# A diffusion block on one core: gate multiplication moved from VectorE to GpSimd, later weight loads, moved quads, raised filler thresholds

## The chip, the cores and the metric

One core of a Trainium2 chip runs the kernel. The metric is device time in microseconds, the median of the runs. The engines are called PE (TensorE, matmul; its weight loads are listed as PEld), ACT (ScalarE), DVE (VectorE), POOL (GpSimd) and SP (SyncE, which here only issues transfers).

## The reference

An attention block and a gated MLP, each with a layer norm, a modulation and a gate computed from a condition vector `c`. 2048 tokens, 640 features, 32 heads of 20, 1536 hidden features, all bfloat16:

```python
mod = (_silu(c) @ w_mod).reshape(c.shape[0], 6, 1, -1)
sa, ca, ga, sb, cb, gb = (mod[:, 0].copy(), ..., mod[:, 5].copy())
h = _layernorm(x, axis=-1) * (1 + ca) + sa
x = x + ga * _A_ref(h, A_wqkv, A_wo)
h = _layernorm(x, axis=-1) * (1 + cb) + sb
x = x + gb * _B_ref(h, B_w_gate, B_w_up, B_w_down)
```

`_A_ref` is softmax attention over all tokens followed by `@ wo`; `_B_ref` is `((h @ w_gate) * (h @ w_up)) @ w_down`.

## The kernel before

The program is written by a planner. Python code builds tasks (an engine, a duration, dependencies, a priority, and sometimes a gate), a greedy simulation puts them into an order for each engine, and `emit_program` writes that order out with semaphores. On the chip every engine runs its list in order. So a constant of the planner, even a duration, can change the order of everything that follows.

**Tiling.** Queries are cut into seven chunks (`CHUNKS`): 512 tokens, then six of 256. In a chunk there are eight items of four heads each. For an item, PE computes scores in units of 512 columns, with four heads in the four row groups of the array (line 1522), and the exponential of a unit is taken in one of two ways.

- ACT takes two units at a time from PSUM and writes `PP` (line 1559). Two pairs of PSUM banks alternate, so that PE can fill one while ACT reads the other.
- A *quad* is four units that go to DVE and POOL instead. DVE writes each unit as a biased int16 into `DB` (line 1583), then builds two terms from the bits in `DSS` (lines 1615 and 1623, `M` and `EX`), and a product of the first term with `DB` is made either by DVE (line 1620) or in four pieces of 512 columns by POOL (line 1635). `QUADS` says how many quads each item of each chunk has.

PE multiplies `PP` and `DSS` with the values (line 2189). At the end of an item DVE transposes and inverts the sums (1715, 1721), POOL (or, for some, DVE) multiplies (1723), DVE transposes back into `OcT` (1732), and SP copies the rows into `Ocp` (1744).

**The suffix of a chunk** (`suffix(ci)`) is out-projection, layer norm and MLP, and it runs as filling work under the next chunk's scores. Its gates let each round of matmuls start only from some number of exponentials on, spread over a share `GATE_F[ci]` of the next chunk; its priorities are 1000 x (ci + 1) upwards, those of the out-projection 1500 lower. `g`, `progress` and `gstart` count exponentials: chunk `ci` starts at `gstart[ci]`, `NG` is their number.

**Weights of the MLP.** Gate and up weights come in twelve column blocks (`fc`) through three buffers `stg` (line 1929, issued by SP). For the last chunk ten of the twelve have buffers of their own, `stx`. The first `nsq` = 5 of these lie in the region of dead queries, the other five in the region of the earlier MLP tiles, so that their loads wait for the MLP of chunk 4. The gate of their loads is `gstart[NC - 1] + 1 + STX_G * fc`, with `STX_G` 3.

**Down weights.** They are loaded once into `wd` (1502), after the last projection has left the region, and multiplied there by the gate `gb` in twelve instructions (1505), one for each row block of 640 columns. All down-projections depend on these.

**Locks.** DVE instructions that use the SBUF port shared with POOL are marked `lk = 1`. The planner does not start them while a POOL task runs that is marked, and the other way round. A POOL task with `lk = 2` also looks ahead: it is not started if a marked DVE task would be ready more than `LKTOL` before its end, and it gets a dependency on the last marked DVE task.

**Fillers.** The planner keeps a sum of PE's activity over the last 3413 ns. Below `FILL_HARD`, and from 20000 ns of the plan on, it puts in matmuls whose result is not used (`zero_fill`, line 2520, adds zeros to an open sum; line 2548 writes a free bank). `HAM_MIN` is the activity below which the planner takes PE to run at half speed. Ahead of fillers, `HOLD` keeps PE free if scores are about to be ready. A value below `FILL_MIN` makes the planner prefer projection and MLP rounds over value matmuls. `STAGE` sets such constants anew for each of the 57 items; what an entry does not name falls back to the global value.

Of the kernel before, what the change touches and what calls it, by code (L numbers as in the profile page):

```python
# [7 lines left out]
ALU = mybir.AluOpType  # L8
# [23 lines left out]
STEAL_END = 66197.894  # L32
STEAL_GAP = 200
HAM_W = 3413.3
HAM_MIN = 3000.0
LKTOL = 300.0


# [92 lines left out]
class Sched:  # L131
# [221 lines left out]
def emit_program(nc, sched, nsem_dma=56):  # L353
# [121 lines left out]


CHUNKS = ((0, 512), (512, 256), (768, 256), (1024, 256), (1280, 256), (1536, 256), (1792, 256))
QUADS = ((0, 4, 3, 3, 3, 4, 4, 4), (1, 2, 1, 2, 1, 2, 1, 2), (2, 2, 1, 2, 2, 2, 1, 2), (2, 2, 2, 2, 2, 2, 2, 2), (2, 2, 1, 2, 2, 2, 1, 2), (2, 2, 1, 2, 2, 2, 1, 2), (2, 1, 2, 2, 2, 1, 2, 0))
SPLITJ = 1
QHALF = ((0, 0), (0, 0))  # L480
TB_GATE = 2
# [2 lines left out]
PV_KEEP = 2  # L484
# [20 lines left out]
GU_ONE = 1  # L505
XCONT = 0
T3_POOL = 1
STX_G, W_ISSUE = 3, 500.0
ZFILL = 1
LATE0, LATE1 = 24.0, 0.2  # L510
HEAD_OUT = 2
NPS = 4
# [22 lines left out]
PREEMPT = 0.0  # L535
PRE_M = 0.3
PV0N = 1
GATE_F = (1.3, 0.5, 0.5, 0.5, 0.5, 0.5, 1.0)
FILL_MIN = 4190.746
FILL_HARD = 3500.0  # L540
FILL_T0, FILL_TH, FILL_MINH = 2300.0, 17000.0, 7500.0
FILL_MODE = 'P'
DUP_MIN = 0.0
# [17 lines left out]
NTERM = 2  # L561

STAGE = {
    0: {"HOLD": 95, "PVMAX": 14, "LKTOL": 300.0, "X_LATE": -179.96, "FILL_MIN": 4462.4, "STEAL_GAP": 200, "PVCAP": 12, "PVTOL": 249, "XBACK": 0, "D_LATE": 16, "TPRIO": 0.75, "EAGER": 9, "PV_KEEP": 2, "XDPRIO": 1.343, "PVMIN": 2, "D_RES": 74, "X_HALF": 0.0},
    1: {"EAGER": 12},
    2: {"DL": 0.376, "XBACK": 4, "EAGER": 3, "X_HALF": 8.9, "HOLD": 90.5, "PVCAP": 11},
    3: {"PVTOL": 91.9, "X_HALF": -35.7, "HOLD": 100.3},
    4: {"PVMIN": 4, "FILL_MIN": 4884.9, "D_RES": 14},
    5: {"PVMIN": 1, "PVMAX": 10},
    6: {"STEAL_GAP": 189.7, "XBACK": 1, "PV_KEEP": 3},  # L570
    7: {"DL": 0.501, "EAGER": 12, "PVTOL": 68.2},
    8: {"PVCAP": 11, "EAGER": 11},
    11: {"DL": 0.443, "X_LATE": 182.1},
    12: {"DL": 0.459, "FILL_MIN": 3951.9, "PVMIN": 5},
    13: {"DL": 0.417, "HOLD": 87.3, "XBACK": 1},
    14: {"D_RES": 37, "FILL_MIN": 4680.6, "LKTOL": 213.0, "EAGER": 11, "D_LATE": 16},
    17: {"HOLD": 80.9, "PVMAX": 8},
    18: {"HOLD": 176.8, "D_LATE": 16},
    19: {"DL": 0.471, "X_HALF": 175.2, "PV_KEEP": 2, "HOLD": 92.4},
    20: {"DL": 0.391, "X_LATE": 12.3},  # L580
    21: {"HOLD": 78.5},
    22: {"EAGER": 9},
    24: {"DL": 0.464, "X_HALF": -92.0, "LKTOL": 267.1},
    25: {"DL": 0.549, "XBACK": 1},
    26: {"DL": 0.411, "FILL_MIN": 3312.8, "PV_KEEP": 2},
    27: {"DL": 0.473},
    28: {"PV_KEEP": 4, "LKTOL": 434.2},
    29: {"X_LATE": -60.4, "PV_KEEP": 3},
    30: {"PVCAP": 8},
    31: {"PV_KEEP": 3, "HOLD": 134.3},  # L590
    32: {"XBACK": 1, "PVMAX": 9, "PVCAP": 17, "PVMIN": 3},
    33: {"DL": 0.442, "X_LATE": -93.2},
    34: {"PV_KEEP": 1, "LKTOL": 261.2},
    35: {"HOLD": 49.4},
    36: {"DL": 0.524},
    37: {"XBACK": 1},
    38: {"PVMIN": 3, "LKTOL": 408.0, "X_LATE": 5.0},
    39: {"X_LATE": -98.7, "PVMAX": 8, "PVTOL": 316.5},
    41: {"X_HALF": 32.3},
    43: {"D_LATE": 13, "X_LATE": 7.1, "X_HALF": 111.5},  # L600
    50: {"FILL_MIN": 4782.5},
    51: {"X_LATE": -53.2, "PVCAP": 11},
    52: {"HOLD": 122.0, "PV_KEEP": 3},
    53: {"X_HALF": -11.3},
    55: {"FILL_MIN": 3839.7, "XBACK": 0, "X_HALF": -89.7, "HOLD": 83.7, "EAGER": 3},
    56: {"LKTOL": 370.4, "PVMIN": 5},
}
XHALF = 1
STG_G0, STG_G, XC_G = 12, -10, -20
X_LATE = -24.052  # L610
X_HALF = 0.0
# [10 lines left out]
def build_kernel(nc, A_x, A_wqkv, A_wo, B_x, B_w_gate, B_w_up, B_w_down, c, w_mod, out):  # L622
    S, D, H, DH = A_x.shape[1], A_x.shape[2], 32, 20
# [6 lines left out]
    NC = len(CHUNKS)  # L630
# [6 lines left out]
    sc = Sched()  # L637
# [64 lines left out]
    gab = alloc("gab", [128, 2, D], BF16)  # L702
# [51 lines left out]
    wd_sb = Sub(late_off, late_size).alloc("wd", [128, FT, D], BF16)  # L754
# [35 lines left out]
    if NALT:  # L790
# [6 lines left out]
        nsq, nsx = nsx, len(stx)  # L797
# [606 lines left out]
    def need(x):  # L1404
        return 13 + 10 * x
# [41 lines left out]
    ev_gb = gab_round(5, 1, need(WM_NEED + .55))  # L1447
# [54 lines left out]
    d_wd = dma("sp", 128 * FT * D * 2, lambda e: e.dma_start(wd_sb[:], wdv[:, :, :]), proj_last, prio=20)  # L1502
    t_wd = []
    for f_ in range(FT):
        t_wd.append(dvl(395, lambda e, f_=f_: e.tensor_tensor(wd_sb[:, f_, :], wd_sb[:, f_, :], gab[:, 1, :],
                                                                ALU.mult), [d_wd] + ev_gb, prio=2.45))
# [83 lines left out]
    for qi, (it, us) in enumerate(dquads):  # L1590
# [36 lines left out]
        if X_POOL and qi % X_POOL == X_POOL - 1 and qi < len(dquads) - X_LAST and all(  # L1627
                dquads[z][0] == it for z in range(qi, min(len(dquads), qi + X_TAIL + 1))):
            st_["xby"] = None
            for x in range(X_PIECES):  # L1630
# [5 lines left out]
                t = Task("pool", w * POOL_NS + 180.0, fxp, [tm, te], prio=2.0 + .1 * qi + .01 * x, name=f"XP.{qi}")  # L1636
# [15 lines left out]
            t = term(fx, [tm, te], TT_2X, "X", src=0, last=True)  # L1652
# [118 lines left out]
    def suffix(ci):  # L1771
# [36 lines left out]
        for tl in range(ntl):  # L1808
# [30 lines left out]
            t = t0 + tl  # L1839
# [80 lines left out]
        for fc in range(FT):  # L1920
            use_x = tail and fc < nsx
            wbuf, dm = [], []
            for w_, wv in enumerate((wgv, wuv)):
                cell = {}
                if use_x:
                    cell["t"] = stx[fc][:, w_, :, :]

                def f(e, wv=wv, fc=fc, cell=cell):
                    return e.dma_start(cell["t"], wv[:, :, fc * 128:(fc + 1) * 128])
                t = dma("sp", int(STG_B * 128 * KD * 128 * 2), f,  # L1930
                        (sfx_done["qdead"] if fc < nsq else first) if use_x else
                        kp_use if ci == 0 else [], prio=16 + ci + .01 * fc, dur=W_ISSUE,
                        gate=int(gstart[NC] - 40) if tail and not use_x else int(gstart[NC - 1]) + 1 + STX_G * fc if tail else max(0, gb + (STG_G0 if ci == 0 else STG_G)))
                if not use_x:
                    t.acq = [(sStg[w_], "s", 1)]

                    def on0(task, cell=cell, w_=w_):
                        cell["i"] = task.slots["s"]
                        cell["t"] = stg[cell["i"]][:, w_, :, :]
                    t.on_start = on0  # L1940
                wbuf.append(cell)
                dm.append(t)
# [102 lines left out]
        for tl in range(ntl):  # L2045
# [5 lines left out]
            for (c_, w) in cuts:  # L2051
# [10 lines left out]
                if tail and TAILX:  # L2062
# [6 lines left out]
                            prio=1))  # L2069
# [8 lines left out]
    for it in range(len(items)):  # L2078
        ci, j = items[it]
# [313 lines left out]
    def pick_pe(t):  # L2393
# [64 lines left out]
        sr = s_ready()  # L2458
        if HOLD and sr is not None and t < sr <= t + HOLD and ring() >= RINGLOW:
            return half_x(t)  # L2460
        if sc.recent(t) < FILL_HARD and t > 20000 and do_fill(t):
            return True
        if sc.recent(t) < FILL_MIN and ring() >= RINGLOW and pick_x(t, True):
            return True
# [161 lines left out]
```

## Time and profile before

| what | us |
|---|---|
| three runs | 805.65, 806.5, 809.9 |
| median | 806.5 |
| the profiled execution | 804.39 |
| its span, as the profile counts it | 802.6 |
| PE busy | 787.8 (98%), 16467 matmuls |
| ACT busy | 764.6 (95%) |
| DVE busy | 691.0 (86%) |
| POOL busy | 390.1 (49%) |

PE's share is modelled from pipelined matmuls and overstates it. The granted PE clock is 1.00 in each stretch of 20 us, 0.99 in the last. In the chain of waits, followed back from the last instruction, PE has 63% of the span, ACT 24%, DVE 8%: neither engine alone sets the time. The DMA engines are busy 95% of the first 20 us, then mostly 10 to 40%.

Idle time is told in the list of groups after the second bar, with the engine and line that ended most of it. The busy time by stage gives, for a stretch of the span, busy microseconds of each engine with the number of instructions in brackets. Times in the timeline and the chain are from the start of the span.

### The profile page before, as it was taken

How to read it: one execution, taken by the hardware profiler on the slowest of the kernel's cores; microseconds unless marked ns; L12 is line 12 of the kernel's file. 1: busy time of each engine (PE TensorE's matmuls, PEld its weight loads, DVE VectorE, ACT ScalarE, POOL GpSimd, SP SyncE). 2: the span in 40 equal slices, each digit the busy share in tenths (PEclk: the TensorE clock that was granted, in tenths of full speed). 3: DMA queues.
4: the chain of work that ended last, by engine and by line, in shares of the span. 5: the costliest groups of instructions: out<-in, count | busy, mean ns of one | idle time of the engine just before them, and what ended most of it. 6: DMA issues, size and time to landing. Idle time of an engine off the chain costs nothing.

```text
span 802.6 us, 37539 instructions
## 1 busy us (share of the span) xinstructions
PE 787.8 (98%) x16467; PEld 376.9 (47%) x16467; DVE 691.0 (86%) x1407; ACT 764.6 (95%) x848; POOL 390.1 (49%) x404
## 2 busy tenths in 40 slices
PE   8999999999999999999999999999999999999998
PEld 4433433332244334444555455554555555455567
DVE  7878887888979789997899999999999899898654
ACT  6899999999999999999999999999999999999951
POOL 3343546476455742457566455663543435465300
PEclk9999999999999999999999999999999999999999
DMA  9843212112232362110042304230431044527300
GB/s 299 245 118 93 52 52 72 53 30 80 84 96 65 85 186 54 29 42 23 23 106 54 72 16 114 54 74 15 115 88 39 24 112 103 109 71 148 87 22 18
DMA packets 154313, 64.65 MB, mean 81 GB/s; under 512 B 116951, under 2 KB 154151, under 8 KB 154151
## 3 DMA queue, kind: packets, MB, share of 16 engines
q1 hardware_dynamic: 153223, 61.10, 30.0%
q8 instruction: 131, 2.15, 1.1%
q10 hardware_dynamic: 928, 1.15, 0.4%
q14 instruction: 31, 0.25, 0.1%
HBM read 50.63 MB, written 8.99 MB: 74 GB/s over the span
## 4 chain that ended last, share of the span: by engine, by line
PE 63%; ACT 24%; DVE 8%; issue 3%; SPq 1%; DMA 0%; POOL 0%; DVEq 0%; ACTq 0%; POOLq 0%
ACT PP L1559 24%; PE ps_all L1522 21%; PE ps_all L972 17%; PE ps_all L2189 14%; PE ps_all L1232 4%; DVE DB L1583 3%; PE ps_all L968 3%; DVE DSS L1623 1%; PE ps_all L2548 1%; DVE DSS L1615 1%; SPq L1744 1%; DVE DSS L1620 1%; PE ps_all L2520 1%; PE ps_all L1129 1%; PE ps_all L1887 1%
## 5 line engine op out<-in xcount | busy, mean ns | idle before, releaser
L1559 ACT ACTIVATE PP<-ps_all 128x1024 bf16<-128x1024 f32 x810 | 747.5, 1097 | 5.2 <-PE ps_all L1522 2.9
L1635 POOL TENSOR_TENSOR DSS<-DB,DSS 128x512 bf16<-128x512 bf16 x288 | 327.3, 1157 | 301.0 <-DVE DSS L1623 239.2
L1583 DVE TENSOR_SCALAR DB<-ps_all 128x512 int16<-128x512 f32 x428 | 285.5, 681 | 49.1 <-PE ps_all L1522 47.2
L1522 PE MATMUL ps_all<-QT,KT 32*128 32x256 bf16 (+2 forms) x3648 | 317.5, 286 | 6.6 <-ACT PP L1559 2.1
L1522 PEld LDWEIGHTS ps_all<-QT,KT 32*128 32x128 bf16 x3648 | 93.4, 92 | 208.0 <-ACT PP L1559 143.8
L2189 PE MATMUL ps_all<-PP,Vf 128*32 128x256 bf16 (+2 forms) x2892 | 161.9, 290 | 0.3 <-DVE Vf L1321 0.2
L972 PE MATMUL ps_all<-h2T,stg 128*32 128x256 bf16 (+2 forms) x2692 | 125.0, 282 | 0.8 <-DVE DB L1583 0.4
L2189 PEld LDWEIGHTS ps_all<-PP,Vf 128*32 128x32 bf16 (+1 forms) x2892 | 55.0, 94 | 75.0 <-issue 66.3
L2189 PE MATMUL ps_all<-DSS,Vf 128*32 128x256 bf16 (+1 forms) x1512 | 87.9, 290 | 0.5 <-DVE DSS L1620 0.3
L972 PEld LDWEIGHTS ps_all<-h2T,stg 128*32 128x32 bf16 x2692 | 61.2, 96 | 29.4 <-issue 22.8
L1623 DVE TENSOR_SCALAR DSS<-DB 128x2048 int16<-128x2048 int16 x107 | 74.1, 693 | 0.8 <-PE ps_all L2189 0.8
L1615 DVE TENSOR_SCALAR DSS<-DB 128x2048 int16<-128x2048 int16 x107 | 73.4, 686 | 0.4
L972 PE MATMUL ps_all<-wd,hprod 128*32 128x320 bf16 (+1 forms) x1340 | 61.7, 282 | 0.2 <-DVE DB L1583 0.2
L1723 POOL TENSOR_TENSOR OTn<-OT,invT 128x256 bf16<-128x256 f32 (+1 forms) x49 | 35.6, 727 | 38.2 <-DVE invT L1721 38.1
L2189 PEld LDWEIGHTS ps_all<-DSS,Vf 128*32 128x32 bf16 x1512 | 35.1, 95 | 22.6 <-issue 12.4
L1620 DVE TENSOR_TENSOR DSS<-DB,DSS 128x2048 bf16<-128x2048 bf16 x35 | 42.7, 1219 | 0.1
L972 PE MATMUL ps_all<-wV,hT 128*32 128x160 bf16 x1280 | 38.9, 234 | 0.6 <-issue 0.4
L972 PEld LDWEIGHTS ps_all<-wd,hprod 128*32 128x32 bf16 x1340 | 30.6, 96 | 14.0 <-issue 9.9
L1715 DVE STREAM_TRANSPOSE OT<-ps_all 128x256 f32<-128x256 f32 (+2 forms) x57 | 27.0, 474 | 11.1 <-PE ps_all L2189 11.0
L1232 PE MATMUL ps_all<-hT,wq 128*32 128x512 bf16 x375 | 31.5, 382 | 0.4 <-DVE DB L1583 0.3
L1232 PE MATMUL ps_all<-hT,wk 128*32 128x512 bf16 (+1 forms) x360 | 31.8, 382 | 0.0
L972 PE MATMUL ps_all<-wo,Ocp 128*32 128x320 bf16 (+1 forms) x644 | 31.2, 284 | 0.5 <-DVE KPB L1244 0.5
(131 smaller groups left out, 536.2 us busy)
## 6 DMA issues: line engine op xcount, KB each, us to landing
stg<-in_B_w_gate_dram SPq DMA_DIRECT2D x74, 160.0 KB
stg<-in_B_w_up_dram SPq DMA_DIRECT2D x74, 160.0 KB
KT<-k_rows SPq DMA_DIRECT2D x112, 32.0 KB
QT<-q_rows SPq DMA_DIRECT2D x48, 64.0 KB
Ocp<-OcT SPq DMA_DIRECT2D x164, 10.0 KB
wm<-in_w_mod_dram SPq DMA_DIRECT2D x3, 800.0 KB
x<-in_A_x_dram SPq DMA_DIRECT2D x7, 320.0 KB
k_rows<-KPA SPq DMA_DIRECT2D x16, 128.0 KB
```

What stands on the lines that cost most here:

```text
L972: return lambda e, b: e.matmul(ps[32 * x:32 * x + 32, b, c0 + o:c0 + o + w], lhs()[:, 32 * x:32 * x + 32], rhs() if w == n else rhs()[:, o ...
L1232: f = [lambda e, b_, k=k, x=x: e.matmul(ps[x:x + min(32, w - x), b_, :], wx[:, k, r0 + x:r0 + min(x + 32, w)], hT[tc][:, k, :], tile_posit ...
L1522: ems.append(lambda e, i=i, kt=kt: e.matmul(dstf()[:, i * u.n:(i + 1) * u.n], KT[32 * u.s:32 * u.s + 32, u.j, kt * 128:(kt + 1) * 128], QT ...
L1559: return e.activation(PPs[g % 2][:, cellp["p"], 0:nu * 512], ps[:, b0:b0 + nu, :].rearrange("p b c -> p (b c)"), AFT.Exp, scale=ESCALE)
L1583: return e.tensor_scalar(DBl[st_["slot"]][:, x * 512:(x + 1) * 512], bank(cell["b"]), EBIAS, 0.0, op0=ALU.add, op1=ALU.max)
L1615: return e.tensor_scalar(DSl[st_["ss"][0]][:, :], DBl[st_["slot"]][:, :], 0x7F, 0x3F00, op0=ALU.bitwise_and, op1=ALU.bitwise_or)
L1620: return e.tensor_tensor(d, DBl[st_["slot"]][:, :].bitcast(BF16), d, ALU.mult)
L1623: return e.tensor_scalar(DSl[st_["ss"][1]][:, :], DBl[st_["slot"]][:, :], 0x7F80, 2, op0=ALU.bitwise_and, op1=ALU.bitwise_or)
L1635: return e.tensor_tensor(d, DBl[st_["slot"]][:, x * w:x * w + w].bitcast(BF16), d, ALU.mult)
L1715: t1 = Task("dve", n * 1.1 + 70, lambda e: e.transpose(OT[:, 0:n], ps[:, item_info[it]["bank"], 0:n].rearrange("p (b q r) -> p b r q", q=3 ...
L1723: f3 = lambda e: e.tensor_tensor(OTn[:, 0:n].rearrange("p (b c r) -> p b r c", c=32, r=2), OT[:, 0:n].rearrange("p (b r c) -> p b r c", c= ...
L2189: ems.append(lambda e, i=i, kt=kt, stt=stt, stp=stp: e.matmul(ps[32 * s:32 * s + mc, bk, 0:u.n], Vf[:, (kt * H + 4 * u.j + s) * VW:(kt * H ...
```

## The change

Six things change, all in the planner's input, and so the order of nearly everything:

- the twelve multiplications of the down weights by the gate go to POOL (`WD_POOL`), with priority 400, later than all other POOL work, and `lk = 2`;
- of the last MLP's ten `stx` blocks, the sixth to the tenth are asked for from 20, 19, 17, 16 and 14 exponentials before the end (`STX_T`, `STX_S`); the planner takes 600 ns instead of 500 for the issue of a gate or up load (`W_ISSUE`);
- chunk 1 has two quads more, chunk 3 two fewer;
- `FILL_HARD` is 3600 instead of 3500 and holds from 16000 ns of the plan (`HARD_FROM`) instead of 20000; `HAM_MIN` is 3100 instead of 3000;
- `GATE_F` of chunk 0 is 0.446 instead of 1.3;
- `STAGE` is another table (its `DL` entries, which place the quads, are the same).

```diff
-HAM_MIN = 3000.0
+HAM_MIN = 3100.0
...
-QUADS = ((0, 4, 3, 3, 3, 4, 4, 4), (1, 2, 1, 2, 1, 2, 1, 2), (2, 2, 1, 2, 2, 2, 1, 2), (2, 2, 2, 2, 2, 2, 2, 2), (2, 2, 1, 2, 2, 2, 1, 2), (2, 2, 1, 2, 2, 2, 1, 2), (2, 1, 2, 2, 2, 1, 2, 0))
+QUADS = ((0, 4, 3, 3, 3, 4, 4, 4), (2, 2, 1, 2, 2, 2, 1, 2), (2, 2, 1, 2, 2, 2, 1, 2), (2, 2, 1, 2, 2, 2, 1, 2), (2, 2, 1, 2, 2, 2, 1, 2), (2, 2, 1, 2, 2, 2, 1, 2), (2, 1, 2, 2, 2, 1, 2, 0))
...
-STX_G, W_ISSUE = 3, 500.0
+STX_G, STX_T, STX_S, W_ISSUE = 3, 20, 1.5, 600.0
 ZFILL = 1
+WD_POOL, WD_PRIO = 1, 400.0
...
-GATE_F = (1.3, 0.5, 0.5, 0.5, 0.5, 0.5, 1.0)
+GATE_F = (0.446, 0.5, 0.5, 0.5, 0.5, 0.5, 1.0)
 FILL_MIN = 4190.746
-FILL_HARD = 3500.0
+HARD_FROM = 16000
+FILL_HARD = 3600.0
...
 STAGE = {
-    0: {"HOLD": 95, "PVMAX": 14, "LKTOL": 300.0, "X_LATE": -179.96, "FILL_MIN": 4462.4, "STEAL_GAP": 200, "PVCAP": 12, "PVTOL": 249, "XBACK": 0, "D_LATE": 16, "TPRIO": 0.75, "EAGER": 9, "PV_KEEP": 2, "XDPRIO": 1.343, "PVMIN": 2, "D_RES": 74, "X_HALF": 0.0},
-    1: {"EAGER": 12},
...
+    0: {"PV_KEEP": 2, "TPRIO": 0.75, "EAGER": 9, "PVMAX": 14, "PVCAP": 12, "X_HALF": 0.0, "LKTOL": 300.0, "STEAL_GAP": 200, "X_LATE": -179.96, "D_RES": 74, "PVMIN": 2, "XBACK": 0, "FILL_MIN": 3463.3, "HOLD": 95, "XDPRIO": 1.343, "PVTOL": 249, "D_LATE": 16},
+    1: {"FILL_MIN": 5357.0, "PVMAX": 4, "D_LATE": 20},
...
     for f_ in range(FT):
-        t_wd.append(dvl(395, lambda e, f_=f_: e.tensor_tensor(wd_sb[:, f_, :], wd_sb[:, f_, :], gab[:, 1, :],
-                                                                ALU.mult), [d_wd] + ev_gb, prio=2.45))
+        fwd = lambda e, f_=f_: e.tensor_tensor(wd_sb[:, f_, :], wd_sb[:, f_, :], gab[:, 1, :], ALU.mult)
+        if WD_POOL:
+            t_wd.append(pool(D * POOL_NS + 180.0, fwd, [d_wd] + ev_gb, prio=WD_PRIO))
+            t_wd[-1].lk = 2
+        else:
+            t_wd.append(dvl(395, fwd, [d_wd] + ev_gb, prio=2.45))
...
-                        gate=int(gstart[NC] - 40) if tail and not use_x else int(gstart[NC - 1]) + 1 + STX_G * fc if tail else max(0, gb + (STG_G0 if ci == 0 else STG_G)))
+                        gate=int(gstart[NC] - 40) if tail and not use_x else int(gstart[NC - 1]) + 1 + STX_G * fc if tail and fc < nsq else
+                        NG - STX_T + int(STX_S * (fc - nsq)) if tail else max(0, gb + (STG_G0 if ci == 0 else STG_G)))
...
-        if sc.recent(t) < FILL_HARD and t > 20000 and do_fill(t):
+        if sc.recent(t) < FILL_HARD and t > HARD_FROM and do_fill(t):
```

More of the change, by code (lines that the diff above doesn't have):

```diff
@@ L563 @@
 STAGE = {
-    0: {"HOLD": 95, "PVMAX": 14, "LKTOL": 300.0, "X_LATE": -179.96, "FILL_MIN": 4462.4, "STEAL_GAP": 200, "PVCAP": 12, "PVTOL": 249, "XBACK": 0, "D_LATE": 16, "TPRIO": 0.75, "EAGER": 9, "PV_KEEP": 2, "XDPRIO": 1.343, "PVMIN": 2, "D_RES": 74, "X_HALF": 0.0},
-    1: {"EAGER": 12},
[L566 to L585, printed above, removed]
-    27: {"DL": 0.473},
[L587 to L605, printed above, removed]
@@ L606 @@
-    56: {"LKTOL": 370.4, "PVMIN": 5},
+    0: {"PV_KEEP": 2, "TPRIO": 0.75, "EAGER": 9, "PVMAX": 14, "PVCAP": 12, "X_HALF": 0.0, "LKTOL": 300.0, "STEAL_GAP": 200, "X_LATE": -179.96, "D_RES": 74, "PVMIN": 2, "XBACK": 0, "FILL_MIN": 3463.3, "HOLD": 95, "XDPRIO": 1.343, "PVTOL": 249, "D_LATE": 16},
+    1: {"FILL_MIN": 5357.0, "PVMAX": 4, "D_LATE": 20},
+    2: {"DL": 0.376, "PV_KEEP": 4, "PVMIN": 1, "D_LATE": 12},
+    4: {"PVMIN": 4, "EAGER": 13, "HOLD": 58.0, "X_LATE": -39.3},
+    5: {"XBACK": 1, "PVCAP": 9, "X_HALF": -69.7},
@@ new lines @@
+    7: {"DL": 0.501, "HOLD": 136.3, "PVMAX": 7},
+    8: {"D_LATE": 15, "PVMIN": 4, "HOLD": 141.6, "XBACK": 1},
+    10: {"X_LATE": -75.7},
+    11: {"DL": 0.443, "HOLD": 85.2, "PVCAP": 10, "XBACK": 1},
+    12: {"DL": 0.459, "HOLD": 108.3, "X_LATE": 6.6},
+    13: {"DL": 0.417, "FILL_MIN": 4787.5, "X_LATE": -4.5},
+    14: {"PVMIN": 6},
+    15: {"X_LATE": 86.8},
+    17: {"PVMIN": 2, "D_LATE": 20, "D_RES": 12},
+    19: {"DL": 0.471, "HOLD": 130.5, "LKTOL": 495.9},
+    20: {"DL": 0.391, "D_RES": 12, "XBACK": 3},
@@ new lines @@
+    23: {"EAGER": 3, "X_HALF": 50.3},
+    24: {"DL": 0.464, "X_HALF": 17.6, "XBACK": 0},
+    25: {"DL": 0.549},
+    26: {"DL": 0.411, "HOLD": 174.0, "PV_KEEP": 2, "X_HALF": -47.1},
+    27: {"DL": 0.473},
+    28: {"EAGER": 2, "FILL_MIN": 3970.7},
+    29: {"D_LATE": 11, "PVCAP": 15, "FILL_MIN": 3969.0},
+    31: {"HOLD": 173.2, "X_HALF": 164.9, "PV_KEEP": 2},
+    32: {"D_RES": 44, "D_LATE": 17, "PVTOL": 349.6},
+    33: {"DL": 0.442, "LKTOL": 876.0, "EAGER": 2, "PVTOL": 223.6},
+    34: {"PVMIN": 7, "PV_KEEP": 3, "X_HALF": 147.4, "PVCAP": 12, "HOLD": 52.6, "D_RES": 27},
@@ new lines @@
+    35: {"X_HALF": 148.7},
+    36: {"DL": 0.524, "D_RES": 8, "PV_KEEP": 3},
+    37: {"X_LATE": 42.7, "D_LATE": 12},
+    39: {"X_LATE": 136.2},
+    40: {"PVCAP": 9},
+    41: {"LKTOL": 414.8, "PV_KEEP": 3},
+    42: {"FILL_MIN": 3229.7},
+    43: {"X_LATE": -87.2},
+    46: {"EAGER": 9, "PV_KEEP": 3, "PVMIN": 2, "HOLD": 119.8},
+    50: {"FILL_MIN": 4797.6, "X_LATE": -35.5, "XBACK": 0},
+    51: {"XBACK": 0, "X_LATE": 8.0},
+    53: {"X_LATE": -38.2},
+    55: {"D_RES": 25, "FILL_MIN": 4778.8},
@@ L607 @@
+    56: {"PVTOL": 497.0, "D_RES": 23, "FILL_MIN": 4847.4},
 }
```

## The prediction

> **What bounds the kernel.** I read the list of costly groups first, then the busy time by stage, then the chain of waits, then single stretches of the timeline. The groups:
>
> ```profile
> L1559 ACT ACTIVATE PP<-ps_all 128x1024 bf16<-128x1024 f32 x810 | 747.5, 1097 | 5.2 <-PE ps_all L1522 2.9
> L1583 DVE TENSOR_SCALAR DB<-ps_all 128x512 int16<-128x512 f32 x428 | 285.5, 681 | 49.1 <-PE ps_all L1522 47.2
> L1623 DVE TENSOR_SCALAR DSS<-DB 128x2048 int16<-128x2048 int16 x107 | 74.1, 693 | 0.8 <-PE ps_all L2189 0.8
> L1615 DVE TENSOR_SCALAR DSS<-DB 128x2048 int16<-128x2048 int16 x107 | 73.4, 686 | 0.4
> L1620 DVE TENSOR_TENSOR DSS<-DB,DSS 128x2048 bf16<-128x2048 bf16 x35 | 42.7, 1219 | 0.1
> L1635 POOL TENSOR_TENSOR DSS<-DB,DSS 128x512 bf16<-128x512 bf16 x288 | 327.3, 1157 | 301.0 <-DVE DSS L1623 239.2
> ```
>
> Line 1559 is ACT's exponential. There are 810, and they hold ACT nearly from end to end. The busy time by stage says where they do not:
>
> ```profile
> 0.00:40.00 40.00, 37.69 (x605) 18.46 (x605) 32.65 (x109) 31.66 (x48) 14.13 (x36) 1.00 0.87 272
> 120.00:440.00 320.00, 315.52 (x6179) 132.51 (x6171) 280.21 (x537) 318.93 (x346) 179.22 (x175) 1.00 0.26 68
> 440.00:774.00 334.00, 329.81 (x7933) 173.86 (x7929) 295.89 (x592) 332.34 (x362) 160.85 (x161) 1.00 0.33 75
> 774.00:803.00 29.00, 25.66 (x419) 22.12 (x417) 16.30 (x47) 4.05 (x11) 1.10 (x2) 1.00 0.06 19
> ```
>
> The columns are the stretch, its length, busy us of PE, weight loads, DVE, ACT and POOL, the granted clock, DMA share and GB/s. ACT idles 2.7 us in the 654 us between 120 and 774. By the start times of the exponentials in the trace, the first begins at 16.35 us, the last at 772.4, and the median step is 0.905 us. So the span is 16.35 to the first, 809 x 0.905 = 732.1 of steps, 24.3 by which steps are longer than that, and 30.2 from the last start to the end: 802.6, and with 1.8 around it the execution's 804.39. Of the 24.3, chunk 0 of the queries has 12.2 (5.5 of it before 40 us, where ACT also evacuates projections), and chunks 1 to 6 have 2.8, 2.1, 2.4, 2.0, 1.4 and 1.4.
>
> PE is the second bound. It always has out-projection and MLP work waiting: the down-projection of chunk 4 ends at 709 us, 31 us after chunk 5's scores ended at 678, and chunk 5's ends just before the last MLP begins:
>
> ```profile
> 777.58 1.68 PE L972 MATMUL ps_all<-wd,hprodt 128*32 128x320 bf16 x44
> 779.53 2.91 PE L968 MATMUL ps_all<-h2Tc,stx 128*128 128x128 bf16 x49 [0.28 <-DVE h2Tc L1877]
> ```
>
> (Start, length, what ran.) Only about 0.3 us lie between them: PE work added earlier can come out there.
>
> **The change, part by part.** The number of exponentials does not change. A quad takes four score units from ACT, and the sums of the table are 25+12+14+16+14+14+12 = 107 before and 25+14+14+14+14+14+12 = 107 after; 810 steps stay, so 732.1 us stay. What can move is the 24.3, the head and the end.
>
> *Down weights off DVE.* Twelve multiplications at 477 ns (line 1505) are 5.7 us of DVE, at 292.7 to 311 us, where DVE is full:
>
> ```profile
> 292.00:356.00 64.00, 63.15 (x1241) 26.40 (x1242) 61.84 (x119) 63.91 (x70) 26.39 (x28) 1.00 0.22 51
> ...
> 293.97 1.17 DVE wd L1505 x3
> ```
>
> The last line is of the chain of waits: three of the twelve are on it, 1.17 us. ACT's steps from 280 to 320 us lose 1.4. The bounds are 0 (the next DVE instruction takes the place) and -2.8 (all of chunk 1's loss); I take the chain's -1.2.
>
> *The same on POOL.* No row has 640 columns there. The piece of line 1635 has 512 in 1157 ns, so 1157 x 640/512 = 1446 ns, and twelve are 17.4 us. From the landing of the weights (by 292.7) to the first down matmul of chunk 0 (356.4) POOL works 26.4 of 64 us, which leaves 37.6: the work hides. Without that cover it is 17.4 us of delay for the first down-projection, behind which PE has chunk 1's out-projection. The multiplications wait for the load and for DVE's last port-locking instruction; behind them in POOL's order stand pieces of line 1635 (PE's value matmuls wait for them) and of 1723 (attention output, then SP's copies into Ocp). The plan holds the two engines apart, but not perfectly, as one stretch of DVE and POOL shows:
>
> ```profile
> 153.87 1.50 POOL L1723 TENSOR_TENSOR OTn<-OT,invT 128x512 bf16<-128x512 f32 x1
> 154.38 1.53 DVE L1623 TENSOR_SCALAR DSS<-DB 128x2048 int16<-128x2048 int16 x1
> 156.63 1.94 ACT L1559 ACTIVATE PP<-ps_all 128x1024 bf16<-128x1024 f32 x2 [0.50 <-PE ps_all L1522]
> ```
>
> The DVE instruction took 1.53 us for a median of 0.683 while POOL worked, and ACT then waited 0.50. Only four of the 214 of lines 1615 and 1623 are longer by over 0.2 us beside 337 large POOL instructions, 1.7 us in all, so twelve more cost 12/337 x 1.7 = 0.1. The bounds are 0 and the second rival's price.
>
> *Quads moved.* A quad is 4 x 681 + 693 + 686 + 1219 x 35/107 = 4.5 us of DVE and two exponentials less. Chunk 1 gets two more (+9.0, less the 5.7), chunk 3 two fewer (-9.0):
>
> ```profile
> 220.00:300.00 80.00, 78.97 (x1518) 32.38 (x1514) 67.46 (x133) 79.85 (x87) 45.05 (x47) 1.00 0.40 108
> 400.00:480.00 80.00, 78.40 (x1848) 40.34 (x1836) 75.12 (x151) 79.20 (x87) 43.21 (x44) 1.00 0.27 62
> ```
>
> DVE is at 84% in the first stretch and 94% in the second, so the load evens out. But the loss does not follow it (2.8 us in chunk 1, 2.4 in chunk 3), so I take 0, between -2.4 and +2.8.
>
> *Late weights.* Ten loads of stx (gate and up for the sixth to tenth of twelve column blocks) move from SP's order at 714.0 to 729.1 us to 20 to 14 exponentials before the end, 754.3 to 759.7. Each holds SP about 0.57 us, 5.7 in all, among these:
>
> ```profile
> 713.99 1.00 SPq L1929 DMA_DIRECT2D stx<-in_B_w_gate_dram  x1
> ...
> 755.42 10.26 SPq L1744 DMA_DIRECT2D Ocp<-OcT  x9
> 768.82 12.23 SPq L2068 DMA_DIRECT2D out_dram<-xckt  x2
> ```
>
> Even if all ten went behind the nine copies, they would be issued by 765.7 + 5.7 = 771.4 and move 1.64 MB, 10 us at the 163 GB/s of the slice around 730: landed about 778 by the slower of the two. The first pair is needed 40 matmuls after 779.53, at 781.9. Where they leave, the MLP of chunk 5 ran without waiting (714.8 to 756.9, as long as chunk 4's 43 us). So 0 on both sides. The copies of item 6 (762 to 765.7) may land 1 or 2 us later than now, but are needed at 772.2.
>
> *Fillers.* Line 2520 has 164 matmuls, 10.2 us busy in the whole span. The threshold rises from 3500 to 3600 and holds from 16 us of the plan. The granted clock is 1.00 in every stretch, so none is needed in this execution. The bounds are 0 and +10.2 (they double); I take +0.3, the gap that the end has. The Trainium skill (TensorE: Matmul & The Clock Gate, "What's actually happening") says that too little PE activity in a free-running window of 3.4 us halves the clock; then fillers would help runs other than the profiled one. No row here shows it.
>
> *GATE_F of chunk 0, 1.3 to 0.446.* Gate and up of chunk 0 run from 264.7, when the last query projection is done, to 351.8, and down from 356.4: the gates (at latest 132 exponentials after chunk 1's start at 214.9, 334 us) are passed before. 0.
>
> *The retuned stage table* redraws the plan. The losses of the sixteen 40-us stretches from 120 to 760 us have a mean of 0.9 and a deviation of 0.37 us; redrawn independently their sum moves by 4 x 0.37 = 1.5. 0, plus or minus that.
>
> Sum: -1.2 + 0.1 + 0.3 = -0.8, so 803.6 beside the execution's 804.39. The median of the runs is 2.1 above that execution: 805.7 with the same spread. I forecast the middle, 804.6, own range 801 to 808.
>
> **Rivals.** *The redrawn plan really is better.* Chunk 0 after 40 us loses 6.7 in 175 us; at chunk 6's rate (1.4 in 94) it would be 2.6, and chunks 1 to 4 at 1.4 each save 3.7: 7.8 in all. Half of it gives 804.4 - 3.9 = 800.5, all of it 796.6. For it: chunks 5 and 6 show that the rate can be had. Against: chunk 0 carries the projections.
>
> *The port.* Each POOL multiplication could hold DVE's locking instructions for its whole length: 17.4 us, against the 2.2 that DVE idles from 292 to 356 plus the 5.7 it is freed of. It decides from 7.9 us on, and all twelve give 804.4 + 9.5 = 813.9. For it: the 1.53 above. Against: four cases in 337. The Trainium skill (SBUF — State Buffer, "Who interferes with whom") says that the two engines share a port pair as an exclusive lock and the second blocks fully; by that rule this is the time when the plan drifts, and the trace agrees where they met.
>
> *More fillers, PE late.* They double, and PE, already behind, ends chunk 5 later: 804.4 + 10.2 - 0.3 = 814.3. It decides from 0.3 us on. Against: a filler goes where PE is starved.
>
> *Weights late at the end.* A load queued behind SP's wait for chunk 5's output (which ends at 781) lands after 783.5, the tenth 8 us later, where 785 is the need: about +7, 811.
>
> That the change does nothing is inside the forecast.
>
> **How the numbers follow.** Chances: forecast 0.50, better plan 0.22, port 0.12, fillers 0.11, late weights 0.05. A measurement of this kernel can tell about 0.5%, 4.0 us: 802.5 and 810.5 are the bounds. Faster: 0.13 of the forecast and 0.22. Same: 0.34 of it, 0.01 + 0.02 + 0.01 of the slow rivals. Slower: 0.03, 0.11, 0.09, 0.04. That is 0.35, 0.38, 0.27. The range, 797.5 to 813, takes most of the better plan and half of the slow cases.
>
> **What would show it.** Right: 810 exponentials; no line 1505 on DVE but twelve of about 1.45 us on POOL, done before the first wd matmul; lengthened steps of 22 to 25 us in sum; ten stx loads at 754 to 766 and no wait of line 968 for a DMA; 29 to 31 us from the last exponential's start. Wrong: the sum of lengthened steps under 20 or over 28, many DVE term instructions over 0.9 us around 300 to 350 us, chunk 5's down matmuls after 780, or line 2520 over 250.

## The result and the profile after

| | before | after |
|---|---|---|
| median of 20 runs each, same chip, us | 806.36 | 810.41 |
| lowest and highest, us | 805.09, 809.9 | 807.27, 816.13 |
| the profiled execution, us | 804.39 | 808.06 |
| its span, us | 802.6 | 806.2 |

The ratio is 1.0046, with a 95% interval of 1.0031 to 1.006: slower by 0.46%, where 0.2% faster was forecast. The direction is wrong and the time is above the forecast's own range of 801 to 808.

The profiled spans differ by 3.6 us. By the start times of the exponentials, the first begins at 16.43 us (16.35 before), 809 steps of 0.905 stay, what single steps take beyond that adds up to 29.7 us (24.3; "long steps" and "loses" below mean this sum), and 28.6 us follow the last start (30.2): +0.1 + 5.4 - 1.6 = 3.9. The other -0.3 is in the steps that are shorter than 0.905, which give back 0.7 us after and 0.4 before. By chunk the 29.7 are 15.0, 4.3, 1.8, 2.1, 2.1, 2.5 and 1.9, so chunk 0 has lost 2.9 more than before and chunk 1 1.5. The groups of the page after:

```profile
L1563 ACT ACTIVATE PP<-ps_all 128x1024 bf16<-128x1024 f32 x810 | 749.4, 1095 | 8.7 <-PE ps_all L2194 3.9
L1639 POOL TENSOR_TENSOR DSS<-DB,DSS 128x512 bf16<-128x512 bf16 x244 | 277.1, 1155 | 307.3 <-DVE DSS L1627 253.9
...
L1624 DVE TENSOR_TENSOR DSS<-DB,DSS 128x2048 bf16<-128x2048 bf16 x46 | 58.1, 1264 | 0.2
```

The lines have moved by four (1563 was 1559). There are 810 exponentials again, with 8.7 us of idle time instead of 5.2. POOL has 244 pieces of products instead of 288, that is 61 quads instead of 72, and DVE has 46 products instead of 35. So eleven products have gone from POOL to DVE, 11 x 1.264 = 13.9 us, more than the 5.7 us it was freed of: DVE is busy for 702.3 us (691.0), POOL for 357.9 (390.1). Two groups of the list of lines after:

```profile
L1505 POOL TENSOR_TENSOR wd<-wd,gab 128x640 bf16<-128x640 bf16 x12 | 16.7, 1396 | 16.1 <-DVE DSS L1627 11.5 <-DVE DSS L1624 4.5
L2525 PE MATMUL ps_all<-ident,Vf 128*32 128x256 bf16 (+1 forms) x160 | 8.3, 297 | 0.0
```

The twelve multiplications are on POOL, from 301.5 to 346.3 us, ahead of the first down matmul at 368.3. Zero-adding fillers are 160 (164 before). The busy time by stage after (us, then busy us of PE, weight loads, DVE, ACT and POOL with counts, granted clock, DMA share, GB/s):

```profile
0.00:40.00 40.00, 36.38 (x568) 17.41 (x568) 32.20 (x107) 31.55 (x48) 13.93 (x36) 1.00 0.88 271
40.00:80.00 40.00, 39.35 (x625) 13.95 (x622) 35.71 (x60) 39.34 (x43) 11.59 (x10) 1.00 0.35 93
80.00:120.00 40.00, 38.49 (x700) 15.56 (x696) 31.20 (x62) 35.08 (x38) 14.51 (x13) 1.00 0.22 57
120.00:440.00 320.00, 316.33 (x6186) 134.00 (x6187) 292.13 (x542) 318.24 (x346) 161.50 (x156) 1.00 0.25 66
440.00:774.00 334.00, 331.34 (x8094) 176.55 (x8089) 292.80 (x589) 333.06 (x362) 155.32 (x155) 1.00 0.34 77
```

and of the kernel before, for the third row:

```profile
80.00:120.00 40.00, 39.25 (x703) 15.19 (x705) 32.52 (x64) 38.33 (x42) 19.06 (x17) 1.00 0.20 53
```

Between 80 and 120 us ACT is busy for 35.1 us and takes 38 instructions, against 38.3 and 42: 3.3 us, most of the difference of the spans. The long steps there are 6.4 us (2.8), while all of 120 to 760 us has 15.6 (14.4). SP's timeline in that stretch after:

```profile
82.37 6.78 SPq L1748 DMA_DIRECT2D Ocp<-OcT  x9
89.19 1.78 SPq L1278 DMA_DIRECT2D q_rows<-KPA  x3
91.02 1.16 SPq L1452 DMA_DIRECT2D q_rows<-Ocp  x2
93.26 2.19 SPq L1300 DMA_DIRECT2D QT<-q_rows  x2
```

and the chain that ended last in that window:

```profile
90.51 2.68 DMA q_rows<-KPA
...
93.26 4.34 DMA QT<-q_rows
97.60 0.05 issue
97.64 0.45 PE ps_all L1526 x4
```

SP issues nine copies of attention output into `Ocp`, which the out-projection first reads at 229.8 us, and only then the query rows and the queries `QT`. The queries land at 97.6 us, and PE, which waited 1.1 us for them, starts the scores there. Before, SP's timeline was:

```profile
83.41 1.63 SPq L1278 DMA_DIRECT2D q_rows<-KPA  x3
...
88.74 0.77 SPq L1744 DMA_DIRECT2D Ocp<-OcT  x1
89.62 0.89 SPq L1300 DMA_DIRECT2D QT<-q_rows  x2
90.56 2.24 SPq L1744 DMA_DIRECT2D Ocp<-OcT  x3
```

The query rows went out at 83.4 and `QT` at 89.6, with one copy between and three behind, and no score waited for a transfer. Two fills of the rows' padding (`q_rows<-Ocp`, 384 KB each) went out at 76.1 and 78.5, while the kernel after has them between the query rows and `QT`. By the semaphores in the trace the first `QT` takes 4.3 us from issue to landing there, 0.3 us behind the second fill, and took 2.2 us before.

The end is 28.6 us, just under the forecast's 29 to 31. Its timeline on PE:

```profile
781.51 1.68 PE L972 MATMUL ps_all<-wd,hprodt 128*32 128x320 bf16 x44
783.12 2.74 PE L968 MATMUL ps_all<-h2Tc,stx 128*128 128x128 bf16 x46
```

No matmul of the last MLP waits for a transfer, though the tenth pair of loads is issued only at 773.4 us, behind five copies and an output. The gain of 1.6 comes from the last chunk's out-projection, of which half now runs between the last scores: 12 of its 24 matmuls start behind the last exponential's start, where 23 did before.

The mean granted clock of an execution is 1.000 in 69 of the 91 executions of the kernel before that were timed beside the experiments (median 805.6 us; the others 808.6) and in 4 of 20 of the kernel after (807.7; the others 810.65). So about 2.1 us of the difference are there at full clock, as far as four executions tell, and the other half comes because most executions of the kernel after run some microseconds at a lower one.

### The profile page after: what moved, and what is told of

Same layout as the page of the kernel before. It is cut to its first block, busy times and chain, and to the rows that moved or that the text cites. A ratio compares the mean times of both kernels' runs of the same rounds, so it can differ in the third digit from the quotient of the medians.

```text
span 806.2 us, 37845 instructions
## 1 busy us (share of the span) xinstructions
PE 791.4 (98%) x16639; PEld 381.7 (47%) x16639; DVE 702.3 (87%) x1409; ACT 764.9 (95%) x845; POOL 357.9 (44%) x372
## 4 chain that ended last, share of the span: by engine, by line
PE 71%; ACT 12%; DVE 11%; DMA 2%; issue 2%; SPq 1%; POOL 0%; DVEq 0%; ACTq 0%
PE ps_all L1526 25%; PE ps_all L972 20%; PE ps_all L2194 17%; ACT PP L1563 12%; PE ps_all L1232 4%; PE ps_all L968 3%; DVE DB L1587 3%; DVE st L1073 1%; DVE DSS L1619 1%; DVE DSS L1627 1%; SPq L1748 1%; DVE hT L1137 1%; PE ps_all L1891 1%; DMA stg<-in_B_w_up_dram 1%; DVE DSS L1624 1%
## 5 line engine op out<-in xcount | busy, mean ns | idle before, releaser
L1639 POOL TENSOR_TENSOR DSS<-DB,DSS 128x512 bf16<-128x512 bf16 x244 | 277.1, 1155 | 307.3 <-DVE DSS L1627 253.9
L2194 PE MATMUL ps_all<-PP,Vf 128*32 128x256 bf16 (+2 forms) x2892 | 164.5, 290 | 0.1
L1624 DVE TENSOR_TENSOR DSS<-DB,DSS 128x2048 bf16<-128x2048 bf16 x46 | 58.1, 1264 | 0.2
L2194 PEld LDWEIGHTS ps_all<-DSS,Vf 128*32 128x32 bf16 x1512 | 36.8, 95 | 20.7 <-issue 10.1
L972 PEld LDWEIGHTS ps_all<-wd,hprod 128*32 128x32 bf16 x1376 | 31.6, 96 | 14.2 <-issue 10.6
L1961 DVE CAST gsb<-ps_all 128x256 bf16<-128x256 f32 x60 | 24.8, 415 | 9.2 <-PE ps_all L972 8.9
L972 PEld LDWEIGHTS ps_all<-wV,hT 128*32 128x32 bf16 x1280 | 24.9, 96 | 15.6 <-issue 9.0
```

Source lines behind the costliest of these rows:

```text
L972: return lambda e, b: e.matmul(ps[32 * x:32 * x + 32, b, c0 + o:c0 + o + w], lhs()[:, 32 * x:32 * x + 32], rhs() if w == n else rhs()[:, o ...
L1624: return e.tensor_tensor(d, DBl[st_["slot"]][:, :].bitcast(BF16), d, ALU.mult)
L1639: return e.tensor_tensor(d, DBl[st_["slot"]][:, x * w:x * w + w].bitcast(BF16), d, ALU.mult)
L2194: ems.append(lambda e, i=i, kt=kt, stt=stt, stp=stp: e.matmul(ps[32 * s:32 * s + mc, bk, 0:u.n], Vf[:, (kt * H + 4 * u.j + s) * VW:(kt * H ...
```

## The experiments

All ratios are against the kernel before on the same chip. "After's plan" means that the order of all engines is the one of the kernel after, except for what is named.

**Down weights on POOL in before's plan, and back on DVE in after's plan.**

```diff
     end = sc.run()
+    for t in t_wd:
+        t.eng = t.ctr = "pool"
```

(The second kernel, made from the one after, has "dve" there.)

> The kernel before, with its plan kept in every engine's order, and only the twelve multiplications of the down weights taken out of DVE's list and put into POOL's at the same place. If moving them to POOL is what costs (the port held, or POOL's pieces behind them late), this kernel is slower than before by 2 us or more, with DVE instructions of lines 1615 and 1623 over 0.9 us between 290 and 315 us. If the redrawn plan costs and not the parts, it stays within 1.2 us of before, on either side.

> The kernel after, with its plan kept, and only the twelve multiplications taken from POOL's list back into DVE's at the same place. If POOL's multiplications cost the changed kernel its 3.7 us, this one comes back to before (ratio 0.998 to 1.002). If the redrawn plan costs, it stays slower: ratio 1.003 to 1.007, the same long steps of the exponentials at 60, 86 to 102 and 293 us.

The first: 813.6 us, ratio 1.0077 [1.005, 1.0103]. Chunk 1 loses 7.5 us in long steps (2.8 before). Two of its DVE instructions:

```profile
296.88 1.59 DVE L1615 TENSOR_SCALAR DSS<-DB 128x2048 int16<-128x2048 int16 x1
298.40 1.64 DVE L1623 TENSOR_SCALAR DSS<-DB 128x2048 int16<-128x2048 int16 x1
```

and a row of its busy time by stage:

```profile
300.00:320.00 20.00, 17.63 (x302) 7.03 (x306) 16.52 (x23) 16.16 (x17) 16.01 (x10) 0.91 0.16 37
```

DVE's term instructions, 0.69 us elsewhere, take 1.4 to 1.9 us four times beside POOL's multiplications, ACT falls to 16.2 of 20 us, and the granted clock to 0.91. So the port costs time when nobody keeps the two apart. This agrees with the rule of the Trainium skill (SBUF — State Buffer, "Who interferes with whom") that the second of the two engines blocks fully. But the rival's sum is not what happened: DVE is held 5.1 us in all (these four and two products of line 1620), not 17.4, and none of the six executions had a mean granted clock of 1.000. That 813.6 lies beside the rival's 813.9 is luck. What it cost that POOL's own pieces stood behind the multiplications was not separated.

The second: 813.4 us, ratio 1.0082 [1.0059, 1.0105]. Taking the work off POOL again makes the kernel after no faster; it is slower by some 3 us by the medians, since after's plan leaves DVE no room for it (280 to 360 us lose 7.4 us, 2.8 after). So taking POOL's multiplications away does not cure the kernel after; that they are not what made it slow follows from the run with the copies moved (below), which keeps them on POOL and is not slow. This run's profile also shows what a wait in the head can do:

```profile
90.00:100.00 10.00, 7.59 (x175) 4.19 (x164) 5.84 (x16) 6.26 (x8) 4.48 (x4) 0.97 0.50 125
100.00:110.00 10.00, 10.00 (x162) 4.07 (x162) 5.84 (x14) 7.43 (x9) 2.80 (x3) 0.69 0.01 2
```

The head is that of the kernel after, but here SP issues `QT` at 94.6 us and PE waits longer for it:

```profile
PE ps_all L1526 <- DMA QT<-q_rows: 2.4, 1, 2.4
```

(total, times, longest). Behind that gap the granted clock is 0.97 and 0.69, that is (0.03 + 0.31) x 10 / 0.5 = 6.8 us at half speed, and the stretch from 80 to 120 loses 9.7 us instead of 6.4.

**The late weights alone, in the kernel before.**

```diff
-STX_G, W_ISSUE = 3, 500.0
+STX_G, STX_T, STX_S, W_ISSUE = 3, 20, 1.5, 500.0
...
-                        gate=int(gstart[NC] - 40) if tail and not use_x else int(gstart[NC - 1]) + 1 + STX_G * fc if tail else max(0, gb + (STG_G0 if ci == 0 else STG_G)))
+                        gate=int(gstart[NC] - 40) if tail and not use_x else int(gstart[NC - 1]) + 1 + STX_G * fc if tail and fc < nsq else
+                        NG - STX_T + int(STX_S * (fc - nsq)) if tail else max(0, gb + (STG_G0 if ci == 0 else STG_G)))
```

> The kernel before with nothing but the later gates of the ten loads; the issue time in the plan stays at 500 ns and the stage table is before's, so the plan differs only from the middle of the last chunk on. If late weights or their transfers cost, the time from the last exponential's start to the end grows from 30.2 us by 1 or more. By the prediction it is 0: ratio 0.999 to 1.001.

> The kernel before with the late weights alone, as in the run of that edit, timed once more, since its interval of 0.9973 to 1.0001 left open whether it is a little faster. If the 0.13% was real, the ratio lies again at 0.998 to 0.9995 with a like interval, and this is the best version; if it was chance, at 0.9995 to 1.002. The trace should be the same as in that run: ten loads at 753 to 765 us, 30.2 us from the last exponential to the end, no wait of the last MLP for a transfer.

805.24 us, 0.9987 [0.9973, 1.0001], and again 805.98, 0.9996 [0.9978, 1.0013]. The ten loads went out at 753.6 to 765.3 us, the time from the last exponential to the end stayed at 30.2. Late weights are worth nothing that can be told here; the first run's 0.13% was not seen again.

**After's plan without fillers.**

```diff
+    gone = {id(t): t for t in sc.all if t.name in ("fill", "zfill") and t.start > 16000}
...
+    sc.order["pe"] = [t for t in sc.order["pe"] if id(t) not in gone]
```

> The kernel after with its plan kept and all fillers that it places after 16000 ns of the plan left out; they add zeros or write a free bank, so the result is the same. If fillers delay PE, the loss of 2.0 and 6.4 us at 40 to 120 us shrinks by 2 or more and the ratio falls to 1.000 or below. If they only fill holes, the ratio stays at 1.003 to 1.006; a granted clock under 1.00 in some stretch would say that they are needed.

810.91 us, ratio 1.0047 [1.0026, 1.0067], the same as with them. But none of the twelve executions reached a mean granted clock of 0.998; their mean is 0.991. Two rows of its busy time by stage:

```profile
80.00:90.00 10.00, 9.68 (x138) 4.11 (x139) 6.28 (x15) 7.24 (x9) 1.05 (x1) 0.56 0.20 53
90.00:100.00 10.00, 10.00 (x237) 5.68 (x230) 8.81 (x20) 6.98 (x8) 0.00 (x0) 1.00 0.48 116
```

From 80 to 90 us PE runs mostly at half speed. So fillers buy clock, and cost about what they buy. They are neither the loss (rival) nor useless (the prediction's "none is needed").

**The nine copies behind the queries, in after's plan.**

```diff
+    late = [t for t in sc.order["sp"] if 80500 < t.start < 87000 and t.prio == 2]
+    q = [t for t in sc.order["sp"] if 91000 < t.start < 92000]
+    sc.all = [t for t in sc.all if t not in late]
+    at_ = max(sc.all.index(t) for t in q) + 1
+    sc.all[at_:at_] = late
```

> The kernel after with its plan kept, and in SP's list only nine copies into Ocp (needed at about 230 us) put behind the query rows and the two loads of QT that stand after them at 89 to 93 us. If the late queries of the fourth item starve PE at 93 to 97.6 us and so cost ACT's wait and, in many executions, the clock, the step lengthened by 0.96 us at 96 us goes, the loss of the stretch from 80 to 120 us falls from 6.4 by 1 to 3 us, more runs are at a clock of 1.000 than the 5 of 20, and the ratio is 1.000 to 1.003. If the parts of the change cost (POOL's multiplications, fillers, quads), it stays at 1.003 to 1.006.

805.94 us, ratio 1.0005 [0.9991, 1.0019]: no loss that can be told is left, by moving nine entries of one list. SP's timeline of this kernel:

```profile
87.50 1.62 SPq L1278 DMA_DIRECT2D q_rows<-KPA  x3
89.17 2.50 SPq L1452 DMA_DIRECT2D q_rows<-Ocp  x2
92.35 1.25 SPq L1300 DMA_DIRECT2D QT<-q_rows  x2
93.64 6.78 SPq L1748 DMA_DIRECT2D Ocp<-OcT  x9
```

The query rows go out 1.7 us earlier, `QT` 0.9 us, and the first `QT` lands 2.5 us earlier, at 95.1 (behind the second fill again, at 94.8); no score waits for a transfer there. What ACT waited for from 40 to 110 us, in the kernel after

```profile
ACT PP L1563 <- PE ps_all L2194: 3.9, 6, 1.4
ACT PP L1563 <- PE ps_all L1526: 1.4, 2, 0.8
```

and with the copies moved

```profile
ACT PP L1563 <- PE ps_all L2194: 3.7, 6, 1.4
ACT PP L1563 <- PE ps_all L1526: 0.5, 1, 0.5
```

(total, times, longest): the waits for late scores shrink by 0.9 us, those behind value matmuls stay. The span is 803.7, the long steps 27.0 us, chunk 0 has 14.2 and chunk 1 3.1 of them. And 11 of 12 executions have a granted clock of 1.000, where the kernel after had 4 of 20. Of 0.0041 x 806 = 3.3 us won back, 1.8 are seen at full clock (805.9 against 807.7), and the rest goes with the clock. (How many executions keep it also varies for one program: the late weights alone had 11 of 12, then 8 of 12.)

**The converse: four copies ahead of the query rows, in before's plan.** All other engines keep their order.

```diff
+    early = [t for t in sc.order["sp"] if 87500 < t.start < 91000 and t.prio == 2]
+    q = [t for t in sc.order["sp"] if 84000 < t.start < 84800 and t.prio == 1.0]
+    sc.all = [t for t in sc.all if t not in early]
+    at_ = sc.all.index(q[0])
+    sc.all[at_:at_] = early
```

> The kernel before, plan and order of PE, ACT, DVE and POOL unchanged; only in SP's list four copies into Ocp (issued at 88.7 and 90.6 to 92.8 us) are put ahead of the three loads of q_rows at 83.4 us. That is the converse of taking nine copies away from in front of the queries in the kernel after. At 0.75 us each they delay the query rows by 3.0 us; QT, which SP issues at 89.6, follows by up to 3.0. Theory (SP's order in front of the queries costs directly and by the clock): PE waits about 1 to 2.5 us for QT around 93 to 96 us, the steps of the exponential grow by 0.5 to 2.5 us in the stretch 80 to 120, fewer executions keep a granted clock of 1.000, ratio 1.001 to 1.005. Rival (the queries had slack enough, and the kernel after lost its time to other parts of the redrawn plan): no wait for QT, ratio 0.999 to 1.001.

809.68 us, ratio 1.0035 [1.0014, 1.0057]. Its times in the trace are about 4 us later than before's, since this execution also met a low clock at 20 us. SP's timeline:

```profile
87.51 2.99 SPq L1744 DMA_DIRECT2D Ocp<-OcT  x4
90.55 2.18 SPq L1278 DMA_DIRECT2D q_rows<-KPA  x3
...
94.69 0.83 SPq L1300 DMA_DIRECT2D QT<-q_rows  x2
```

ACT's timeline, where ACT stood 2.11 us for scores:

```profile
98.46 1.94 ACT L1559 ACTIVATE PP<-ps_all 128x1024 bf16<-128x1024 f32 x2 [2.11 <-PE ps_all L1522]
101.45 1.94 ACT L1559 ACTIVATE PP<-ps_all 128x1024 bf16<-128x1024 f32 x2 [1.05 <-PE ps_all L2189]
```

and the busy time by stage:

```profile
90.00:100.00 10.00, 7.77 (x168) 3.91 (x166) 7.18 (x19) 6.96 (x8) 3.86 (x4) 0.94 0.21 60
100.00:110.00 10.00, 9.90 (x189) 4.17 (x181) 7.04 (x16) 8.14 (x10) 4.94 (x5) 0.88 0.01 2
```

With three microseconds of copies in front of the queries PE stands for 2.2 us, up to 98.0. The view of waits names no cause, but by its semaphore the first `QT` landed at 97.9. Right behind the gap PE runs (0.06 + 0.12) x 10 / 0.5 = 3.6 us at half speed by these rounded rows; the stretch from 98.89 to 102.30 alone has a clock of 0.50. From 80 to 120 us 6.2 us are lost (2.8 before), about what the kernel after loses, but part of it here is clock, which the profiled execution of the kernel after kept. 4 of 12 executions have a granted clock of 1.000; their median is 806.9, 1.3 above that of the kernel before at full clock. Taking copies away (0.41%) and putting them in (0.35%) move the time by about the same amount in opposite directions: SP's order in the head is the cause, at full clock and through the clock. The rival, that the queries had slack enough, falls.

**The port, kept apart for all POOL work.** In the kernel after, POOL's multiplication 1727 met DVE's 1627 at 59 us:

```profile
59.00 1.53 DVE L1627 TENSOR_SCALAR DSS<-DB 128x2048 int16<-128x2048 int16 x1
```

```diff
-            elif task.lk == 2 and self.lk_last is not None and self.lk_last.done > self.t - 3000.0:
+            elif self.lk_last is not None and self.lk_last.done > self.t - 3000.0:
```

> The kernel after with every order kept; POOL's multiplication at the end of an item (line 1727) now also waits for the last port-locking DVE instruction that the plan puts ahead of it, as POOL's other pieces do. If the overlap at 58 to 60 us (DVE 1.05 and 1.53 us for 0.68) costs, these two fall to 0.7 or less beside it, the 0.65 us of ACT at 60 us goes, and the ratio falls by 0.0005 to 0.0015 to about 1.0035. If not, it stays at 1.0046.

> Both of the last two edits in the kernel after. If the changed kernel is slower because its plan of the first chunk meets these two delays that the planner does not know, the effects add: ratio 0.998 to 1.002. If they are only symptoms, 1.003 or more.

> The kernel before with the later gates of the ten loads (ratio 0.9987 alone) and the same wait at the end of an item. DVE's 1.53 us at 154 us and the 0.72 us of ACT behind it go, and PE's least busy stretch there is filled, so that fewer runs fall under a clock of 1.000: ratio 0.996 to 0.9985. If the overlap costs nothing, 0.9987 again.

The wait does what it says, by DVE's timeline of the first of these:

```profile
58.77 0.68 DVE L1627 TENSOR_SCALAR DSS<-DB 128x2048 int16<-128x2048 int16 x1
```

The stretch from 40 to 80 us loses 1.3 us instead of 2.0. This profiled execution also shows in place what the one of the kernel after does not. SP's order is the same, nine copies first; PE waits 1.8 us for `QT`, up to 97.4, the granted clock is 0.50 from 99.89 to 103.30, and the stretch from 80 to 120 us loses 8.1 us instead of 6.4. On after's plan the kernel takes 808.64 us, 1.0032 [1.0015, 1.0049]; with the copies moved too 806.33, 1.0008 [0.9987, 1.0029]; on before's plan with late weights 804.61, 0.9997 [0.998, 1.0014]. Beside the kernels without the wait (1.0046, 1.0005, 0.9987) each difference is inside the intervals, and the gain in clock that was expected did not come (7 of 12 executions at 1.000 in each of the last two, where the same kernels without the wait had 11 of 12).

**One part of the change alone, planned anew: the stage table, and the quads.** `STAGE` or `QUADS` of the kernel after in the kernel before, as in the diff of the change; two executions each.

> The kernel before with the new stage table alone; quads, gates, fillers, late weights and down weights stay. The prediction had the table at 0 plus or minus 1.5 us as an independent redraw. Theory (a table is fitted to the rest of the input; the two cannot be priced one by one): clearly slower, by 8 to 25 us, ratio 1.01 to 1.03. Rival (the table is a redraw like any other): within 4 us, 0.995 to 1.005.

> The kernel before with the two quads moved from chunk 3 to chunk 1, and nothing else. The prediction had this at 0, between -2.4 and +2.8 us. Theory (fitted table): slower by 5 to 15 us, ratio 1.006 to 1.02, the loss at the end or in chunks 1 to 3. Rival (the load of DVE decides): within 3 us, with chunk 1 losing more and chunk 3 less.

The table alone: 831.99 us, ratio 1.0323 [1.0298, 1.0349]; long steps of 39.7 us, and 41.7 us from the last exponential to the end (30.2). The quads alone: 819.44 us, 1.0167 [1.0143, 1.0192], long steps of 39.7 us, 8.4 of them in chunk 1. One step of ACT there is worth 3.5 us:

```profile
296.93 3.77 ACT L1559 ACTIVATE PP<-ps_all 128x1024 bf16<-128x1024 f32 x4 [3.47 <-PE ps_all L2189]
```

and the chain just ahead of it runs through DVE, with the down weights in its middle:

```profile
292.76 1.13 DVE DSS L1620
293.90 0.40 DVE wd L1505
294.30 0.61 DVE hprod L1994
294.91 0.04 issue
294.95 1.48 PE ps_all L972 x24
```

The table alone also puts the copies in front of the queries, by SP's timeline:

```profile
82.40 7.32 SPq L1742 DMA_DIRECT2D Ocp<-OcT  x9
89.76 2.43 SPq L1276 DMA_DIRECT2D q_rows<-KPA  x3
...
94.02 2.57 SPq L1298 DMA_DIRECT2D QT<-q_rows  x2
```

PE waits 1.9 us for `QT`, the granted clock is 0.50 from 99.41 to 102.82, and from 80 to 120 us 8.4 us are lost. With the quads alone that stretch loses 2.8, as before, and SP has the query rows first. So of the six parts the table is enough to bring the loss in the head.

Neither of the two kernels is a redraw of a few tenths: a table is fitted to the rest of the input, and the parts of this change have no price one by one. In the kernel after the two together, with the down weights off DVE, lose 4.3 us in chunk 1.

## Why the prediction was wrong

**What held.** 810 exponentials and 732.1 us of steps stayed. The down weights on POOL took 16.7 us for an expected 17.4 and hid. The late weights are 0, in the change and twice alone. With `GATE_F` alone the program comes out the same, instruction for instruction: 0. Fillers cost nothing net. Of the rivals, the better plan, more fillers and late weights at the end did not happen. The port rival's mechanism is real, but not its price (DVE held 5.1 us where 17.4 were worked out, in before's plan), and in the plan of the kernel after no term instruction of DVE near the multiplications takes over 0.9 us.

**The step that failed** is "The retuned stage table redraws the plan ... 0, plus or minus that", with 1.5 us. The 1.5 was drawn from the sixteen stretches of 120 to 760 us, and there it held: 15.6 us of long steps against 14.4. It left out the head, where queries and keys reach the scores through SP's in-order list, and the redraw cost 3.6 us in the one stretch from 80 to 120. The runs put in its place: nine copies ahead of the queries there, which the new table brings by itself (8.4 us lost in that stretch for 2.8) and which, moved back, take the ratio from 1.0046 to 1.0005. The prediction had looked at SP's queue only at the end, past 714 us.

**The second half of the loss** has its step too: "The granted clock is 1.00 in every stretch, so none is needed in this execution." True of that execution, and of the profiled one after, yet the plan decides how often the clock holds. The rule that the prediction cited from the Trainium skill (TensorE: Matmul & The Clock Gate, "What's actually happening") was set aside, as no row showed it. Rows show it now: four profiled executions, in which PE stood for 1.8 to 2.4 us there, have a clock of 0.50 from 0.3 to 2.4 us behind the gap on, three of them for one stretch of 3.4 us and one for two (99.38 to 106.21 us, with the down weights back on DVE). The Trainium skill speaks there of an idle window of about 3.4 us; here 1.8 to 2.4 us of standing came before it.

**Smaller terms.** "Down weights off DVE, -1.2" did not come: 280 to 320 us lose 2.2 instead of 1.4. DVE is busy there for 35.4 us (35.8 before), so other work has taken the freed time; over the whole execution eleven products moved from POOL to DVE. What makes the stretch slower than before was not shown. The quads' 0 stands in sum only with the table that goes with them: chunk 3 gained 0.3 and chunk 1 lost 1.5. The end's gain of 1.6 was not foreseen. The four terms of the prediction's span add up to 803.0, not to the 802.6 behind the colon; the 0.4 are the steps shorter than 0.905, and the forecast does not rest on it.

**What stays open.** With the copies moved, 80 to 120 us still lose 5.2 us against 2.8; ACT's waits there are for score units that PE reaches behind value matmuls, and it was not tried to redraw that. The two fills ahead of `QT` were not moved alone, so their share in the delay is not known; with four copies and no fill right ahead of it PE stood too. Chunk 1's gain of 1.2 us in that run has no cause that a run has shown; in the kernel after PE stood 0.6 us at 292.7 for nothing that the trace names. How little activity halves the clock was not measured: a gap of 1.1 us was not followed by it in one execution, one of 1.8 us was in another.

No version beats both kernels: the best, before with late weights, is at 0.9987 and 0.9996, with 1 inside both intervals.

## What to carry to other kernels

When an order is made anew, look first at the stage with least slack, often the head, and at each in-order issue queue there: what was put ahead of the transfer that is waited for next? Some 2 us of standing on TensorE were followed by 3.4 to 6.8 us at half clock, and the one profile of a kernel can miss it; so compare the granted clock over all executions. Do not price the parts of a change that were fitted together as if they were independent.

## What was not expected of the hardware

- A copy of 8 to 20 KB into `Ocp` holds SP's issue for about 0.75 us (nine in 6.78), and so every load behind it.
- Gaps of 1.8, 1.9, 2.2 and 2.4 us in the matmuls were followed by 3.4 us at half clock, the last by 6.8; behind one of 1.1 us, in the profiled execution of the kernel after, the clock stayed at 1.00.
- Where POOL and DVE meet at the port, a DVE instruction of 0.69 us takes 1.4 to 1.9 us.
